# First expert of a retention and mixture-of-experts kernel: the order of its second half

## The chip, the cores and the metric

One core of a Trainium2 chip runs the whole program. The metric is the device time of one execution in microseconds (us). A core has TensorE (PE in the rows; PEld is its weight load), VectorE (DVE), ScalarE (ACT), GpSimd (POOL) and SyncE (SP). SP and POOL also issue the transfers here: SP the plain loads and the transpositions, POOL the indirect gathers and scatters.

## What is computed

```python
def _attn_ref(q, k, v):                    # B, H, S, D = 8, 8, 576, 64
    scores = np.matmul(q, k.transpose(0, 1, 3, 2)) / np.sqrt(D)
    gamma = 1.0 - 2.0 ** (-5.0 - np.arange(H))
    rel = pos[:, None] - pos[None, :]
    Dmat = np.where(rel >= 0, gamma[:, None, None] ** rel[None, :, :], 0.0)
    return np.matmul(scores * Dmat[None], v)

def _moe_ref(x, expert_emb, tau, w1, w2):  # N, D, E, F = 4608, 512, 8, 1024
    xn, en = rows of x and expert_emb divided by (norm + 1e-6)
    logits = xn @ en.T / tau
    expert_idx = argmax(logits, axis=1)
    probs = softmax(logits)
    for e in range(E):
        mask = expert_idx == e
        h = np.maximum(x[mask] @ w1[e], 0.0)
        out[mask] = probs[mask, e, None] * (h @ w2[e])
```

The result of the retention, with the heads side by side, is x. Each token goes to one expert, and its row is scaled by that expert's probability, the gate.

## The kernel before, in words

All is in one function, `retention_moe`. The retention runs first and writes x to a table in HBM (xd). Routing gives every expert five tiles of 128 slots (0 to 4). For an expert e the tokens' rows are gathered by an indirect transfer (`gather`, L379), turned by a DMA transposition on SP's queue (`turn`, L405) and put together from 16-bit halves on ScalarE (`join`, L416). The gates are gathered by five more indirect transfers, 128 numbers each (`gather_gates`, L392), from a table gd that `gates_out` (L254) writes through SP.

Numbers are 32 bits wide, and TensorE multiplies in a reduced form. So every operand is split into a high part (ScalarE copies and rounds it: `whi` L989 and `Split.hi` for weights, `xhi0` L429 and `xhi` L461 for x, `out0_hi` L997 for the middle layer) and a remainder (VectorE subtracts: `wlo` L992, `Split.lo`, `xlo0` L433, `xlo` L466, `out0_lo` L1001), and a product is three matmuls: high by high, high by low, low by high. `mm` (L127) issues all of them.

Expert 0 computes its first product directly: `mm1_in` (L471) makes one of eight groups of 128 columns of the middle layer, 12 matmuls, for tiles 0 to 2 first (q = 0) and then, once their x is there, for tiles 3 and 4 (q = 1, 256 columns). The second product, `mm2` (L1066), takes 24 matmuls of 512 columns a tile, called in pairs of groups; `evac` (L1081) scales the tile by its gates on ScalarE and `scatter` (L1087) writes it on POOL's queue. Experts 1 to 7 run in a loop (from L1296) and compute the first product by seven products of combined quarters (`products`, L1048). Their operands are sums of quarters of w1 (S1 to S4, `sumS1` and so on on VectorE, L977 to L987) and of x (`xsums`, L449), split like the rest. The quarter loads of w1 are `wload` (L963); `wn.load` brings w2, 512 KB a piece.

The order is written out by hand: inside `manual_schedule` every engine issues its instructions in the order of the program's text, and an instruction that waits holds everything behind it on its engine or queue. Lines on different engines don't order each other; only data and free buffers do. So the place of a line in the text counts only among the lines of the same engine. Buffers that matter here: `graw` has three (a turn of tiles 3 and 4 of expert 1 takes one as well), `wraw` has three for all weight loads, PSUM banks pa hold the groups of `mm1_in` in turn (four), and ys two.

The stretch that the change touches is L1133 to L1266: the end of expert 0's first part (L1133 to L1157), tiles 0 and 1 of its second product with the preparation of tiles 3 and 4 among them (L1160 to L1193), the second part of its first product (the loop at L1194), and tiles 2 to 4 of the second product (L1211 to L1266), beside which expert 1's x and weights are got ready. `sum_beyond` (L510) adds up, in 14 small instructions on VectorE, how many tiles the overflow code at the end has to treat; its result is read only by expert 7's turn of the loop (L1299) and behind it.

Of the kernel before, what the change touches and what calls it, by code (L numbers as in the profile page):

```python
# [97 lines left out]
def retention_moe(ctx: ExitStack, tc: tile.TileContext, qk, kv, embT, tau, w1, w2, cst, out):  # L98
# [155 lines left out]
    def gates_out():  # L254

        ps = psm.tile([P, 512], F32, name="m")
        tr(ps[:, :P], tok_all, ident)
        rows = my.tile([P, DM], F32, name="y")
        nc.vector.tensor_copy(rows[:NT, :P], ps[:NT, :P])
        nc.sync.dma_start(out=gd[:, :].rearrange("(t p) o -> t (p o)", p=P), in_=rows[:NT, :P])  # L260
# [115 lines left out]
    xg, gts = {}, {}  # L376
# [15 lines left out]
    def gather_gates(e, tiles=range(CT)):  # L392
        if e not in gts:
            gts[e] = mg.tile([P, CT], F32, name="gt")
        g = gts[e]
        for i in tiles:
            a = _slot(e, i)
            nc.gpsimd.indirect_dma_start(  # L398
                out=g[:, i : i + 1],
                out_offset=None,  # L400
                in_=gd[:, :],
                in_offset=bass.IndirectOffsetOnAxis(ap=gid[:, a : a + 1], axis=0),
            )

    def turn(e, i):  # L405

        if e and i > 2:
            t, u = gr.tile([P, RW], F32, name="graw"), (gx, xsf[:, 2 * NP * HW :])[i - 3]
            xg[e, i] = t
        else:  # L410
            t = u = xg[e, i]
        nc.sync.dma_start_transpose(
            out=t[:, XO : XO + DM].bitcast(U16).rearrange("p (c n) -> p c n", n=P), in_=u[:, :DM].bitcast(U16)
        )

    def join(e, i, copy=nc.scalar.copy):  # L416

        t = xg[e, i]
        copy(  # L419
            t[:, :DM].bitcast(U16).rearrange("p (n h) -> p h n", h=2),  # L420
            t[:, XO : XO + DM].bitcast(U16).rearrange("p (h n) -> p h n", h=2),
        )
# [6 lines left out]
    def xhi0(i):  # L429
        u, x = rows0(i)  # L430
        nc.scalar.copy(x[:, 0], u)  # L431
# [495 lines left out]
    with ExitStack() as moe:  # L927
# [35 lines left out]
        def wload(e, n):  # L963

            i, j = int(n[1]) - 1, int(n[2]) - 1
            t = raw[n] = wr.tile([P, RW], F32, name="wraw")[:, :1024].rearrange("p (d n) -> p d n", d=2)
            nc.sync.dma_start(
                out=t,
                in_=w1[e][j * 256 : (j + 1) * 256, i * 512 : (i + 1) * 512].rearrange("(d p) n -> p d n", p=P),
            )  # L970
# [18 lines left out]
        def whi(n):  # L989
            nc.scalar.copy(wop[n][:, 0], raw[n])  # L990

        def wlo(n):  # L992
            nc.vector.tensor_tensor(  # L993
                out=wop[n][:, 1], in0=raw[n], in1=wop[n][:, 0].bitcast(F32), op=ALU.subtract
            )

        def out0_hi(f, q, ps):  # L997
            o, n = ((0, C0), (C0, C1))[q]
            nc.scalar.activation(hs[:, 0, f, o : o + n], ps[:, :n], AF.Relu)
# [66 lines left out]
        def mm2(ps, i, fs, n=0, step=DM, begin=None, end=None):  # L1066

            for f in fs:
                for k, (a, c) in enumerate(((0, 0), (0, 1), (1, 0))):
                    mm(  # L1070
                        ps[:, :step],
                        hs[:, a, f, i * P : (i + 1) * P],
                        w2t[:, c, f, n : n + step],
                        start=(f == begin and k == 0),
                        stop=(f == end and k == 2),
                        skip_group_check=True,
                    )
# [55 lines left out]
        mm1_in(5, 0, q0[5])  # L1133
        out0_hi(4, 0, q0[4])
        out0_lo(4, 0, q0[4])
        wn.lo(1)
        turn(0, 3)
        wload(1, "A11")
        mm1_in(6, 0, q0[6])
        on(prow)  # L1140
        gates_out()
        gather_gates(0)
        turn(0, 4)
        out0_hi(5, 0, q0[5])
        wn.hi(2)
        out0_lo(5, 0, q0[5])
# [12 lines left out]
        on(prow)  # L1159
        mm2(b0[0], 0, (0, 1), begin=0)  # L1160
        count_beyond()
        whi("A11")
        mm2(b0[0], 0, (2, 3))
        wlo("A11")
        join(0, 3)
        mm2(b0[0], 0, (4, 5))
        xhi0(3)
        join(0, 4)
        xlo0(3)
        xg.pop((0, 3))  # L1170
        gather(1, 1)
        gather(1, 4)
        mm2(b0[1], 1, (0, 1), begin=0)
        xhi0(4)
        sumS3()
        mm2(b0[1], 1, (2, 3))
        xlo0(4)
        xg.pop((0, 4))
        sumS1()
        mm2(b0[0], 0, (6, 7), end=7)  # L1180
        evac(0, 0, b0[0])
        scatter(0, 0)
        whi("S3")
        gather(1, 2)
        turn(1, 1)
        mm2(b0[1], 1, (4, 5))
        wlo("S3")
        whi("A22")
        gather_gates(1)
        mm2(b0[1], 1, (6, 7), end=7)  # L1190
        evac(0, 1, b0[1])
        scatter(0, 1)
# [1 line left out]
        for f in range(NF):  # L1194
            ps = pa[f % 4]
            mm1_in(f, 1, ps)
            out0_hi(f, 1, ps)
            if f in (2, 4, 6):
                join(1, f // 2 - 1)
            if f in (3, 5, 7):  # L1200
                xsums(1, f // 2 - 1)
            out0_lo(f, 1, ps)
            if f in (3, 5, 7):
                xhi(1, f // 2 - 1, "a")
            if f in (4, 6):
                xlo(1, f // 2 - 2, "a")
            if f == 1:
                wlo("A22")
        sumS2("A22")
        wload(1, "A12")  # L1210
        mm2(b0[2], 2, (0, 1), begin=0)  # L1211
        xhi(1, 0, "bc")
        xlo(1, 2, "a")
        xlo(1, 0, "bc")
        xg.pop((1, 0))
        turn(1, 3)
        mm2(b0[2], 2, (2, 3))
        xhi(1, 1, "bc")
        xlo(1, 1, "bc")
        xg.pop((1, 1))  # L1220
        turn(1, 4)
        mm2(b0[2], 2, (4, 5))
        whi("S1")
        wlo("S1")
        wn = Split(1, 1, w2f)
        wn.load(0)
        mm2(b0[2], 2, (6, 7), end=7)
        evac(0, 2, b0[2])
        scatter(0, 2)
        xhi(1, 2, "bc")  # L1230
        mm2(b0[3], 3, (0, 1), begin=0)
        whi("A12")
        xlo(1, 2, "bc")
        xg.pop((1, 2))
        mm2(b0[3], 3, (2, 3))
        whi("S2")
        wlo("A12")
        sumS4()
        mm2(b0[3], 3, (4, 5))
        join(1, 3)  # L1240
        wlo("S2")
        wn.load(1)
        mm2(b0[3], 3, (6, 7), end=7)
        evac(0, 3, b0[3])
        scatter(0, 3)
        xhi(1, 3, "ab")
        xsums(1, 3)
        mm2(b0[4], 4, (0, 1), begin=0)
        xhi(1, 3, "c")
        join(1, 4)  # L1250
        xlo(1, 3, "abc")
        xg.pop((1, 3))
        mm2(b0[4], 4, (2, 3))
        xhi(1, 4, "ab")
        xsums(1, 4)
        sum_beyond()
        mm2(b0[4], 4, (4, 5))
        xhi(1, 4, "c")
        whi("S4")
        xlo(1, 4, "abc")  # L1260
        xg.pop((1, 4))
        mm2(b0[4], 4, (6, 7), end=7)
        evac(0, 4, b0[4])
        scatter(0, 4)
        wlo("S4")
        wn.load(2)  # L1266


        def outs_mid(fs, X, Y):
# [26 lines left out]
        for e in range(1, NE):  # L1296
# [151 lines left out]
            if more:  # L1448
                wlo("S4")
                wnext.load(2)  # L1450
            mm2(o[3], 3, (6, 7), end=7)
            evac(e, 3, o[3])
            scatter(e, 3)
# [7 lines left out]
            wn = wnext  # L1461
# [174 lines left out]
```

## Time and profile before

| | us |
|---|---|
| three runs | 580.13, 582.66, 584.71 |
| median | 582.66 |
| the profiled execution's own time | 582.66 |
| its span, first to last instruction | 580.8 |
| TensorE busy in it | 560.1 (96%) |
| VectorE, ScalarE, POOL busy | 402.2, 353.2, 207.4 |
| mean granted clock of TensorE | 0.991 |

Times inside the span are counted from its start. The first expert's stretch runs from about 154 to 223, each later expert takes some 50. In a timeline a row gives start, length, engine, line, operation, what it writes and reads, shapes and count, and in brackets how long the engine stood idle before it and what ended that. "issue" is a wait for nothing that the profile shows. [...] Ends of matmuls are modelled, their starts are recorded.

### The profile page before, as it was taken

What the parts mean: (1) busy time and instruction counts of PE and PEld (TensorE: products, weight loads), DVE (VectorE), ACT (ScalarE), POOL (GpSimd) and SP (SyncE); (2) the same over time, 40 slices, a digit from 0 to 9 for tenths busy, and PEclk for the clock granted to TensorE, in tenths of its full rate; (3) what the DMA queues carried; (4) which work ended last, traced back from release to release, by engine and by line L of the source; (5) the groups of instructions that cost most, each with busy time, mean ns of one, the idle gap of its engine ahead of it and who ended that gap; (6) DMA issues with size and microseconds to landing.
All of it is one profiled execution on the core that took longest, in us unless ns stands there. A gap on an engine that the chain in (4) does not pass through costs nothing.

```text
span 580.8 us, 13121 instructions
## 1 busy us (share of the span) xinstructions
PE 560.1 (96%) x5156; PEld 502.5 (87%) x5156; DVE 402.2 (69%) x880; ACT 353.2 (61%) x640; POOL 207.4 (36%) x188
## 2 busy tenths in 40 slices
PE   8999999998999898999999999999999999999995
PEld 7888888887897778988998998899799889889985
DVE  2776787877686486896698488669868848975400
ACT  2344355553665377676778578677877856776411
POOL 3763333217343715006504611640570362070021
PEclk9999999999999989999999999999999999999998
DMA  8999999999358545936744593584575459262011
GB/s 294 417 356 365 343 358 357 373 322 196 122 167 196 127 128 189 205 74 181 227 92 138 191 212 87 169 249 84 146 243 121 109 166 273 71 163 84 2 45 41
DMA packets 83067, 111.53 MB, mean 192 GB/s; under 512 B 48135, under 2 KB 48427, under 8 KB 82992
## 3 DMA queue, kind: packets, MB, share of 16 engines
q1 hardware_dynamic: 75312, 90.55, 52.7%
q0 software_dynamic: 7680, 19.95, 10.4%
q8 instruction: 51, 0.84, 0.6%
q14 instruction: 24, 0.20, 0.1%
HBM read 81.10 MB, written 19.94 MB: 174 GB/s over the span
## 4 chain that ended last, share of the span: by engine, by line
PE 71%; issue 11%; DVE 8%; ACT 5%; DMA 2%; POOL 2%; POOLq 0%; ACTq 0%; SPq 0%
PE pa L127 27%; PE po L127 21%; PE pst L127 14%; PE prow L127 7%; PE pa L131 2%; ACT graw L419 2%; PE prow L131 1%; DMA graw<-graw 1%; DVE graw L454 1%; POOL out L1089 1%; DVE w0f L993 1%; DMA graw<-xd,gid 1%; DVE pm L662 1%; DVE hs L1022 1%; ACT w0f L990 1%
## 5 line engine op out<-in xcount | busy, mean ns | idle before, releaser
L1089 POOL DMA_INDIRECT out<-y,sid x40 | 42.5, 1063 | 237.6 <-ACT y L1085 217.0
L127 PE MATMUL po<-w2f,hs 128*128 128x512 f32 x408 | 97.4, 397 | 3.2 <-issue 3.2
L127 PEld LDWEIGHTS po<-w2f,hs 128*128 128x128 f32 x408 | 78.2, 192 | 20.6 <-issue 4.3
L127 PE MATMUL pst<-w2f,hs 128*128 128x512 f32 (+1 forms) x336 | 78.4, 382 | 0.0
L193 DVE TENSOR_TENSOR w2f<-wraw,w2f 128x1024 fp32r<-128x1024 f32 x32 | 39.3, 1227 | 53.4 <-ACT w2f L189 45.2
L127 PEld LDWEIGHTS pst<-w2f,hs 128*128 128x128 f32 x336 | 61.0, 188 | 11.4
L645 POOL TENSOR_TENSOR kvt<-kvt,cs 128x512 f32<-128x512 f32 x35 | 38.7, 1111 | 57.6 <-DMA kvt<-kv 52.7
L398 POOL DMA_INDIRECT gt<-gd,gid x40 | 50.2, 1255 | 20.1 <-issue 11.9
L419 ACT COPY graw<-graw 128x1024 uint16<-128x1024 uint16 x37 | 50.3, 1360 | 2.7 <-DMA graw<-graw 1.9
L127 PE MATMUL pa<-xxf,w0f 128*128 128x296 f32 (+2 forms) x348 | 50.3, 296 | 1.2 <-ACT xxf L431 0.9
L127 PEld LDWEIGHTS pa<-xxf,w0f 128*128 128x128 f32 x348 | 47.6, 188 | 1.9 <-ACT xxf L431 1.3
L662 DVE TENSOR_TENSOR pm<-pa,tri 128x512 f32<-128x512 f32 x64 | 40.1, 682 | 9.4 <-PE pa L127 9.3
L127 PE MATMUL prow<-w2f,hs 128*128 128x512 f32 x192 | 46.0, 389 | 0.0
L127 PE MATMUL pa<-qkt 64*128 64x128 f32 x576 | 42.3, 281 | 1.4 <-DVE t L295 0.7
L127 PEld LDWEIGHTS prow<-w2f,hs 128*128 128x128 f32 x192 | 36.0, 188 | 7.5
L385 POOL DMA_INDIRECT graw<-xd,gid x26 | 32.6, 1254 | 24.4 <-DVE L_all L799 13.6
L127 PEld LDWEIGHTS pa<-qkt 64*128 64x128 f32 x576 | 37.4, 187 | 4.1 <-DVE t L295 1.1
L464 ACT CAST xxf<-graw 128x128 fp32r<-128x128 f32 x70 | 31.7, 459 | 14.3 <-DVE graw L454 12.6
L454 DVE TENSOR_TENSOR graw<-graw 128x128 f32<-128x128 f32 x140 | 34.4, 286 | 7.8 <-ACT graw L419 6.6
L127 PE MATMUL pa<-xsf,w0f 128*128 128x296 f32 (+2 forms) x240 | 39.5, 315 | 0.0
L127 PEld LDWEIGHTS pa<-xsf,w0f 128*128 128x128 f32 x240 | 36.6, 189 | 0.3 <-DVE xsf L435 0.2
L127 PE MATMUL po<-pm,kvt 128*64 128x128 f32 (+1 forms) x640 | 34.9, 263 | 0.0
(196 smaller groups left out, 1102.1 us busy)
## 6 DMA issues: line engine op xcount, KB each, us to landing
wraw<-w SPq DMA_DIRECT2D x64, 512.0 KB
qkt<-qk SPq DMA_DIRECT2D x36, 512.0 KB
kvt<-kv SPq DMA_DIRECT2D x32, 512.0 KB
xd<-xw SPq DMA_DIRECT2D x36, 256.0 KB
kvt<-kv SPq DMA_DIRECT2D x4, 256.0 KB
gt<-gd,gid POOLq DMA_INDIRECT x40
out<-y,sid POOLq DMA_INDIRECT x40
graw<-xd,gid POOLq DMA_INDIRECT x26
```

The costliest lines, as they stand in the source:

```text
L127: pe[:] = [nc.tensor.matmul(*args, **kw)]
L131: pe[:] = [nc.tensor.transpose(*args, **kw)]
L193: nc.vector.tensor_tensor(out=self.to[:, 1, c * 1024 : (c + 1) * 1024], in0=self.raws.pop(c), in1=hi.bitcast(F32), op=ALU.subtract,)
L385: return nc.gpsimd.indirect_dma_start(out=t[:, :DM].bitcast(U16), out_offset=None, in_=xd[:rows, :], in_offset=bass.IndirectOffsetOnAxis(a ...
L398: nc.gpsimd.indirect_dma_start(out=g[:, i : i + 1], out_offset=None, in_=gd[:, :], in_offset=bass.IndirectOffsetOnAxis(ap=gid[:, a : a + 1 ...
L419: copy(t[:, :DM].bitcast(U16).rearrange("p (n h) -> p h n", h=2), t[:, XO : XO + DM].bitcast(U16).rearrange("p (h n) -> p h n", h=2),)
L454: nc.vector.tensor_tensor(out=v[:, 2 * k : 2 * k + 2], in0=a, in1=b, op=ALU.subtract)
L464: nc.scalar.copy(x[:, 0], u)
L645: eng.tensor_tensor(out=v, in0=v, in1=gneg[:, t % KT].unsqueeze(2).broadcast_to([P, H, D]), op=ALU.mult)
L662: nc.vector.tensor_tensor(out=pm[:, h], in0=banks[h].rearrange("p (c n) -> p c n", c=NP), in1=m.unsqueeze(1).broadcast_to([P, NP, P]), op= ...
L990: nc.scalar.copy(wop[n][:, 0], raw[n])
L1089: sc = nc.gpsimd.indirect_dma_start(out=out[:, :], out_offset=bass.IndirectOffsetOnAxis(ap=sid[:, a : a + 1], axis=0), in_=ys[i], in_offse ...
```

## The change

Nothing that is computed changes; no instruction is added or left out. Lines move:

- In the first part `wn.lo(1)` goes behind `gates_out()`, and the load of A11 for expert 1 behind `turn(0, 4)`.
- Among tiles 0 and 1 of the second product the joins and splits of tiles 3 and 4 go ahead of the splits of A11, `gather(1, 2)` and `turn(1, 1)` ahead of the first scatter, and `gather_gates(1)` leaves.
- In the second part of the first product only tile 0 of expert 1 is joined and summed; `sumS2`, the load of A12 and tile 0's remainder come earlier.
- Among tiles 2 to 4 of the second product tiles 1 and 2 of expert 1 are joined, summed and split, then tiles 3 and 4 as later experts do it; S2's split comes earlier, `wn.load(0)` now ahead of `turn(1, 4)`.
- The gates of expert 1 are gathered behind the scatters of tiles 3 and 4, and `sum_beyond` runs in the loop at e = 1, behind `wlo("S4")`.

```diff
--- before.py
+++ after.py
@@ -1133,14 +1133,14 @@
         mm1_in(5, 0, q0[5])
         out0_hi(4, 0, q0[4])
         out0_lo(4, 0, q0[4])
-        wn.lo(1)
         turn(0, 3)
-        wload(1, "A11")
         mm1_in(6, 0, q0[6])
         on(prow)
         gates_out()
+        wn.lo(1)
         gather_gates(0)
         turn(0, 4)
+        wload(1, "A11")
         out0_hi(5, 0, q0[5])
         wn.hi(2)
         out0_lo(5, 0, q0[5])
@@ -1159,34 +1159,33 @@
         on(prow)
         mm2(b0[0], 0, (0, 1), begin=0)
         count_beyond()
-        whi("A11")
+        join(0, 3)
         mm2(b0[0], 0, (2, 3))
-        wlo("A11")
-        join(0, 3)
-        mm2(b0[0], 0, (4, 5))
         xhi0(3)
         join(0, 4)
         xlo0(3)
         xg.pop((0, 3))
         gather(1, 1)
         gather(1, 4)
+        mm2(b0[0], 0, (4, 5))
+        xhi0(4)
+        whi("A11")
+        xlo0(4)
+        xg.pop((0, 4))
+        gather(1, 2)
         mm2(b0[1], 1, (0, 1), begin=0)
-        xhi0(4)
+        wlo("A11")
         sumS3()
         mm2(b0[1], 1, (2, 3))
-        xlo0(4)
-        xg.pop((0, 4))
+        whi("S3")
+        turn(1, 1)
         sumS1()
         mm2(b0[0], 0, (6, 7), end=7)
         evac(0, 0, b0[0])
         scatter(0, 0)
-        whi("S3")
-        gather(1, 2)
-        turn(1, 1)
         mm2(b0[1], 1, (4, 5))
         wlo("S3")
         whi("A22")
-        gather_gates(1)
         mm2(b0[1], 1, (6, 7), end=7)
         evac(0, 1, b0[1])
         scatter(0, 1)
@@ -1195,75 +1194,80 @@
             ps = pa[f % 4]
             mm1_in(f, 1, ps)
             out0_hi(f, 1, ps)
-            if f in (2, 4, 6):
-                join(1, f // 2 - 1)
-            if f in (3, 5, 7):
-                xsums(1, f // 2 - 1)
+            if f == 2:
+                join(1, 0)
+            if f == 3:
+                xsums(1, 0)
             out0_lo(f, 1, ps)
-            if f in (3, 5, 7):
-                xhi(1, f // 2 - 1, "a")
-            if f in (4, 6):
-                xlo(1, f // 2 - 2, "a")
             if f == 1:
                 wlo("A22")
-        sumS2("A22")
-        wload(1, "A12")
+            if f == 4:
+                xhi(1, 0, "a")
+            if f == 5:
+                sumS2("A22")
+                wload(1, "A12")
+                xlo(1, 0, "a")
         mm2(b0[2], 2, (0, 1), begin=0)
         xhi(1, 0, "bc")
-        xlo(1, 2, "a")
         xlo(1, 0, "bc")
         xg.pop((1, 0))
         turn(1, 3)
+        join(1, 1)
         mm2(b0[2], 2, (2, 3))
-        xhi(1, 1, "bc")
-        xlo(1, 1, "bc")
-        xg.pop((1, 1))
-        turn(1, 4)
-        mm2(b0[2], 2, (4, 5))
+        xsums(1, 1)
         whi("S1")
+        xhi(1, 1, "abc")
         wlo("S1")
         wn = Split(1, 1, w2f)
         wn.load(0)
+        xlo(1, 1, "abc")
+        xg.pop((1, 1))
+        turn(1, 4)
+        join(1, 2)
+        mm2(b0[2], 2, (4, 5))
+        whi("S2")
+        xsums(1, 2)
+        xhi(1, 2, "abc")
+        wlo("S2")
+        xlo(1, 2, "abc")
+        xg.pop((1, 2))
         mm2(b0[2], 2, (6, 7), end=7)
         evac(0, 2, b0[2])
         scatter(0, 2)
-        xhi(1, 2, "bc")
         mm2(b0[3], 3, (0, 1), begin=0)
         whi("A12")
-        xlo(1, 2, "bc")
-        xg.pop((1, 2))
-        mm2(b0[3], 3, (2, 3))
-        whi("S2")
         wlo("A12")
         sumS4()
+        wn.load(1)
+        join(1, 3)
+        mm2(b0[3], 3, (2, 3))
+        xhi(1, 3, "ab")
+        xsums(1, 3)
         mm2(b0[3], 3, (4, 5))
-        join(1, 3)
-        wlo("S2")
-        wn.load(1)
+        join(1, 4)
+        xlo(1, 3, "ab")
+        xhi(1, 3, "c")
+        xhi(1, 4, "ab")
+        xsums(1, 4)
+        xlo(1, 3, "c")
+        xg.pop((1, 3))
         mm2(b0[3], 3, (6, 7), end=7)
         evac(0, 3, b0[3])
         scatter(0, 3)
-        xhi(1, 3, "ab")
-        xsums(1, 3)
-        mm2(b0[4], 4, (0, 1), begin=0)
-        xhi(1, 3, "c")
-        join(1, 4)
-        xlo(1, 3, "abc")
-        xg.pop((1, 3))
-        mm2(b0[4], 4, (2, 3))
-        xhi(1, 4, "ab")
-        xsums(1, 4)
-        sum_beyond()
-        mm2(b0[4], 4, (4, 5))
+        gather_gates(1, (0, 1, 2))
         xhi(1, 4, "c")
-        whi("S4")
         xlo(1, 4, "abc")
         xg.pop((1, 4))
+        mm2(b0[4], 4, (0, 1), begin=0)
+        mm2(b0[4], 4, (2, 3))
+        whi("S4")
+        wlo("S4")
+        wn.load(2)
+        mm2(b0[4], 4, (4, 5))
         mm2(b0[4], 4, (6, 7), end=7)
         evac(0, 4, b0[4])
         scatter(0, 4)
-        wlo("S4")
-        wn.load(2)
+        gather_gates(1, (3, 4))
 
 
         def outs_mid(fs, X, Y):
@@ -1448,6 +1452,8 @@
             if more:
                 wlo("S4")
                 wnext.load(2)
+            if e == 1:
+                sum_beyond()
             mm2(o[3], 3, (6, 7), end=7)
             evac(e, 3, o[3])
             scatter(e, 3)
```

## Rows read from the trace of the kernel before

**Rows 1.** Waits of TensorE over the span: in total, times, longest (us).
```profile
PE po L127 <- issue: 3.4, 6, 1.4
PE pa L127 <- DVE xsf L469: 1.9, 1, 1.9
```

**Rows 2.** Timeline of TensorE: start, length, engine, what [idle before].
```profile
143.39 1.10 PE L127 MATMUL po<-qkt,T 64*64 64x128 f32 x32
...
174.40 1.55 PE L127 MATMUL po<-w2f,hs 128*128 128x512 f32 x6
...
186.54 0.38 PE L127 MATMUL pa<-xxf,w0f 128*128 128x256 f32 x1 [0.90 <-ACT xxf L431]
187.26 11.42 PE L127 MATMUL pa<-xxf,w0f 128*128 128x256 f32 x95 [0.34 <-DVE xxf L435]
198.94 0.40 PE L127 MATMUL po<-w2f,hs 128*128 128x512 f32 x1 [0.26 <-issue]
...
203.86 6.89 PE L127 MATMUL po<-w2f,hs 128*128 128x512 f32 x19 [1.36 <-issue]
210.58 5.62 PE L127 MATMUL pst<-w2f,hs 128*128 128x512 f32 x24
...
221.48 0.31 PE L127 MATMUL pa<-xsf,wxf 128*128 128x320 f32 x1
223.69 1.88 PE L127 MATMUL pa<-xsf,wxf 128*128 128x320 f32 x11 [1.89 <-DVE xsf L469]
```

**Rows 3.** Busy time by stretch: length, engines, granted clock (PEclk), DMA share.
```profile
198.70:210.60 11.90, 8.75 (x25) 6.22 (x25) 6.65 (x19) 5.77 (x12) 2.75 (x3) 0.71 0.22 53
210.60:221.50 10.90, 10.90 (x50) 9.00 (x48) 9.29 (x21) 8.92 (x15) 2.13 (x2) 1.00 0.80 229
221.50:223.70 2.20, 0.31 (x3) 0.01 (x1) 1.89 (x12) 1.56 (x3) 0.36 (x1) 1.00 0.00 0
```

The engines stand in the order PE, PEld, DVE, ACT, POOL.

**Rows 4.** Timeline of ScalarE.
```profile
181.62 1.05 ACT L990 CAST wxf<-wraw 128x1024 fp32r<-128x1024 f32 x1 [6.09 <-DMA wraw<-w]
182.57 1.36 ACT L419 COPY graw<-graw 128x1024 uint16<-128x1024 uint16 x1
...
184.48 1.35 ACT L419 COPY graw<-graw 128x1024 uint16<-128x1024 uint16 x1
...
203.89 0.38 ACT L999 ACTIVATE hs<-pa 128x256 fp32r<-128x256 f32 x1 [4.53 <-remote]
```

**Rows 5.** Timeline of VectorE.
```profile
189.89 0.42 DVE L1003 SCALAR_TENSOR_TENSOR hs<-pa,hs 128x256 fp32r<-128x256 f32 x1 [0.41 <-ACT hs L999]
...
221.59 1.52 DVE L517 TENSOR_TENSOR ovs<-ovs,ovf 128x1 f32<-128x1 f32 x8
...
223.22 0.42 DVE L469 TENSOR_TENSOR xsf<-graw,xsf 128x256 fp32r<-128x256 f32 x1
...
277.99 1.23 DVE L193 TENSOR_TENSOR w2f<-wraw,w2f 128x1024 fp32r<-128x1024 f32 x1 [6.79 <-ACT w2f L189]
```

**Rows 6.** The chain that ended last, 170 to 230: start, length, what.
```profile
174.83 7.69 DMA graw<-graw
```

**Rows 7.** Timeline of POOL.
```profile
182.11 0.95 POOL L398 DMA_INDIRECT gt<-gd,gid  x1 [8.20 <-DMA gd<-y]
...
194.80 0.95 POOL L398 DMA_INDIRECT gt<-gd,gid  x1 [0.30 <-issue]
...
201.05 1.01 POOL L1089 DMA_INDIRECT out<-y,sid  x1 [0.30 <-issue]
...
224.80 1.65 POOL L385 DMA_INDIRECT graw<-xd,gid  x1 [0.30 <-DVE xxf L469]
```

**Rows 8.** Timeline of SP's queue.
```profile
236.78 6.12 SPq L412 DMA_TRANSPOSE graw<-graw  x3
```

**Rows 9.** Groups of VectorE, 186 to 224, by shape: count, busy us, mean ns.
```profile
L454 DVE TENSOR_TENSOR graw<-graw 128x128 f32<-128x128 f32 x20 | 5.0, 289 | 3.4 <-ACT graw L419 3.2
...
L993 DVE TENSOR_TENSOR w0f<-wraw,w0f 128x1024 fp32r<-128x1024 f32 x3 | 3.7, 1220 | 0.4 <-ACT w0f L990 0.4
```

## The prediction

> **What bounds the kernel now.** The waits of TensorE come first. The reader is to see how few there are: over the whole span the longest groups are 3.4 us that end with "issue" and 1.9 us behind VectorE's remainders of xsf [rows 1]. Both lie where the diff works, the first expert's second half. The second view is TensorE's timeline of that stretch [rows 2]. It begins at 174.40 with the second product (24 matmuls of 512 columns a tile, 48 for tiles 0 and 1). A tile in the clear takes from 210.58 to about 216.03, 5.45 us or 0.227 us a matmul, so tiles 0 and 1 are through at 174.40 + 48 x 0.227 = 185.3, with a matmul of count_beyond at about 185.5. The second part of the first product (96 matmuls) could start there. TensorE issues one at 186.54 and the other 95 from 187.26; at 11.2/95 = 0.1175 us each, 96 could end at 185.5 + 11.3 = 196.8 and end at 198.5: 1.7 us lost. Tile 2 should take 5.45 us and takes from 198.5 to 210.58, 12.1 us: 6.6 us lost, part because five matmuls (24 less 19) trickle out between 198.94 and 203.86, part because the 19 from 203.86 take 6.89 us, 0.36 us each. The products of expert 1 begin with one matmul at 221.48 and the other eleven at 223.69: 2.1 us. In all 10.4 us.
>
> [...] Fourth, ScalarE [rows 4] and VectorE [rows 5]. ScalarE stands in whi("A11") until 181.62, and only then, in its order, come the joins and splits of tiles 3 and 4, which the waiting product reads. Its evacuation of the sixth of the eight groups (203.89) has waited 4.53 us, though by TensorE's rows that group was issued by 187.26 + 71 x 0.1175 = 195.6. So TensorE is held from inside the 96 matmuls on, by something that no row names.
>
> **Part 1, joins of expert 0 before whi("A11"); wn.lo(1), A11's load and the gates.** Before, the chain stands 7.69 us behind tile 4's transposition [rows 6], whose data lies behind A11's load in SP's queue; A11's 512 KB land first (181.62) and the join starts after its split, at 182.57 [rows 4]. Afterwards the load is issued behind the transposition. From the start of tile 4's join (184.48) to the 95 matmuls (187.26) it takes 2.8 us. If the transposition lands no earlier than 182.5, and the join of tile 3 is done by then, the product can start at 185.3, before 185.5; with A11's data out of the way it lands earlier. So the 1.7 us go in either case. Bounds: 0 (the transposition late by as much) to 1.7; I take 1.7, the row being that of the chain itself. VectorE does the gates' copy before wn.lo(1) and so three evacuations some 0.6 us later (an estimate); the second product reads the last of them only with tile 0's last pair, at 174.4 + 30 x 0.227 = 181.2, some 4 us later: nothing, or 0.6 if that cover is gone. whi("A11") now waits for a load that is one transposition later (about 2 us, from 236.78 and 6.12 us for three [rows 8]), and whi("S3"), evac(0, 0), whi("A22") and the first relu stand behind it. That relu's remainder now starts at 189.89 [rows 5]; with four banks TensorE needs the first bank back at 185.5 + 4 x 1.41 = 191.1. Slack 0.8 us; cost 0, at worst 1.
>
> **Part 2, joins, sums and splits of expert 1.** Before, three joins lie inside the 96 matmuls; afterwards one. The splits go to tiles 2 to 4 of the second product. Between the end of the 96 and expert 1's products each engine has this to do: VectorE was busy 6.65 + 9.29 + 1.89 = 17.8 us from 198.70 to 223.70, of which the three last remainders (1.3), sumS2 (1.2) and sum_beyond (2.3) go elsewhere: 13.0. ScalarE was busy 5.77 + 8.92 + 1.56 = 16.3, less three relus (1.2) and whi("S4") (1.0), which the first product pair doesn't need: 14.1. TensorE has 3 x 5.45 = 16.4. From the release at 203.9 to 223.2 the two needed 19.3 us for about 16.6 busy, a share of 0.86; so 13.0 becomes 15.1 and 14.1 becomes 16.4: a tie with TensorE. As tile 4's join, sums, split and remainder alternate between the two engines, I take a wait of 1.0 us at expert 1's first product, between 0 and 4 (the boundary's 2.1 doubled). On SP, turn(1, 4) is now behind wn.load(0), 512 KB, which waits for wlo("S1"). It waits for tile 1's remainders: from 197 on a join of 1.36 us, four sums of 0.29, wlo("S1") of 1.22 [rows 9] and the remainders around them, so it is issued near 202.7 (an estimate); its join is wanted once ScalarE has done two joins and three splits more, near 208. Those 5 us hide it, if the transposition takes less.
>
> **Part 3, expert 1's gates behind the last scatters.** Before, five gathers of gates from 194.80 to 200.74, 1.25 us each, lie beside the 96 matmuls [rows 7]. Afterwards POOL has there only three gathers of x and two scatters; the fifth gather of x runs before the first scatter, and turn(1, 1) and turn(1, 2) follow it. The gates get 3 places behind scatter(0, 3) and 2 behind scatter(0, 4), so POOL's queue holds scatter(0, 4) and expert 2's five gathers by up to 5 x 1.25 = 6.3 us. Those gathers start at 224.80, 1.3 us after the products, and the transposition that reads the first starts only at 236.78 [rows 7, 8]. Some 10 us of cover: nothing, or what exceeds it.
>
> What the trickle is worth hangs on this part, and the trace before has no row for its cause. Bounds: 6.6 us (it goes) to 0 (it stays), and below 0 if it grows (rival 3). For its going: it occurs once, where gates, transpositions of x and the fast matmuls come together; it ends at 203.86, about 2 us after POOL's last instruction of that burst; the other gate gathers, from 182.11 on, lie beside the slow matmuls, and expert 1's gathers of x beside products without a trickle. In the new order POOL's burst is five instructions of 1.25 us beside the 96 matmuls instead of ten. I take 6.6.
>
> [...]
>
> **Part 4, sum_beyond a stage later.** Eight additions of 1.52 us from 221.59 on and six small ones, some 2.3 us in all, stood ahead of tile 4's remainder at 223.22, for which the products wait [rows 5]: 2.1 us go. Behind expert 1's wlo("S4") VectorE has 6.79 us idle up to 277.99; the 2.3 us fit. Cost 0, 2.3 if that cover were gone. What is late next is the wait of part 2.
>
> **Sum.** 1.7 + 6.6 + 2.1 - 1.0 = 9.4 us. The profiled execution took 582.66 us, span 580.8 and 1.9 around it, and is the median of the three runs shown. Everything behind expert 1's first product is TensorE back to back, so the gain is kept: 582.7 - 9.4 = 573.3 us.
>
> **Rivals.**
> 1. The trickle doesn't hang on the gates and stays; the change does not do what it might. If the sixth of the eight groups is again released about 1.7 us earlier than now, 202.2, the last remainders and sumS2 are done near 205, and 13.0 and 14.1 us at a share of 0.86 put the products at 220.3 instead of 223.6: 3.3 us, 579.4. For it: DMA is at 0.22, so no transfer stands in the way, and the transpositions still run beside the fast matmuls. Against: the list above.
> 2. The end of ScalarE's queue becomes the bound: turn(1, 4) behind wn.load(0) takes the 7.69 us of the chain's row instead of the 5 that are hidden, and wn.load(0) as much as 1.5 ahead of it. Its join stands ahead of tile 4's splits and evac(0, 3): 4.2 us more at the products, 577.5; with a stretch at the lower clock (19 x (0.36 - 0.23) = 2.6 us) 580.1.
> 3. Slower: the trickle grows. The transpositions come earlier and nearer together, and if the second product issues all of tile 2 in the way that five matmuls show now (4.92/5 = 0.98 us instead of 0.227), tile 2 takes 23.6 us instead of 12.1; less the 3.3 of rival 1 that is 8.2 us lost, 590.9. It decides from a trickle 3.3 us longer than now, some four or five matmuls more. For it: nothing names the cause. Against: fewer POOL instructions and a burst that ends earlier.
>
> **How the numbers follow.** The forecast has 0.55, rival 1 0.28, rival 2 0.10, rival 3 0.07. About 1% (5.8 us) is what a measurement of this kernel can tell from no change. The forecast is faster by more; of rival 1 some 0.06 (a trickle that shrinks); rivals 1 and 2 else lie within: faster 0.61, same 0.32, slower 0.07. The range begins with no wait at the boundary and 1.8 us for runs (the runs shown differ by about 2 us from their median): 570.5. It ends with rivals 1 and 2: 580.5.
>
> **What would show it.** Right: the 96 matmuls start by 185.7 in one piece; ScalarE's joins of tiles 3 and 4 stand before A11's split; tile 2 takes 5.5 us, with no clock under 1.00 up to expert 1; the products start between 213 and 215; sum_beyond fills idle time behind expert 1's wlo("S4"). Wrong: a trickle with "issue" beside the transpositions, a second stretch at 0.5, a product that waits over 3 us for xsf, or expert 2's joins waiting for late gathers.

## The result, and the profile after

The changed kernel takes 574.54 us (median of 4 runs, 573.13 to 576.07), the kernel before 582.34 us (4 runs, 580.13 to 584.71): ratio 0.9854, 95% interval 0.9815 to 0.9894, so 7.8 us faster. The forecast was 573.3 us. The sum was nearly right, in part by luck; the experiments show that its terms were not, since two of the obstacles stand side by side in time and can't be added.

The profiled execution took 576.07 us (span 574.3), the highest of its four. First TensorE's waits (total, times, longest, us), where [rows 1] stood:

```profile
PE pa L127 <- issue: 2.1, 4, 0.9
...
PE po L127 <- issue: 0.9, 3, 0.4
```

The wait for VectorE's xsf is gone, and that with "issue" at po is down from 3.4 to 0.9, none of it in this stretch. Of the 2.1 us at pa, 1.2 us (0.53 + 0.20 + 0.43) stand in the 96 matmuls of 256 columns; the fourth wait lies far ahead of them. TensorE's timeline, beside [rows 2]:

```profile
176.12 1.55 PE L127 MATMUL po<-w2f,hs 128*128 128x512 f32 x6
...
187.20 6.61 PE L127 MATMUL pa<-xxf,w0f 128*128 128x256 f32 x55
194.34 0.53 PE L127 MATMUL pa<-xxf,w0f 128*128 128x256 f32 x3 [0.53 <-issue]
195.07 0.28 PE L127 MATMUL pa<-xxf,w0f 128*128 128x256 f32 x1 [0.20 <-issue]
195.78 4.87 PE L127 MATMUL pa<-xxf,w0f 128*128 128x256 f32 x37 [0.43 <-issue]
200.49 5.61 PE L127 MATMUL po<-w2f,hs 128*128 128x512 f32 x24
205.93 5.60 PE L127 MATMUL pst<-w2f,hs 128*128 128x512 f32 x24
...
216.81 1.92 PE L127 MATMUL pa<-xsf,wxf 128*128 128x320 f32 x12
...
220.34 1.92 PE L127 MATMUL pa<-xsf,w0f 128*128 128x320 f32 x12
```

The second product starts 1.72 us later than before (176.12 against 174.40). Most of that arose in the retention, where this execution ran some microseconds at the lower clock; it isn't owed to the change: the start lies between 171.74 and 177.03 in the fourteen traces of this document. The busy time by stretch (length, busy time of PE, PEld, DVE, ACT, POOL, granted clock, DMA share, GB/s), of the kernel before and then of the changed one:

```profile
9.00:13.00 4.00, 3.83 (x77) 3.33 (x75) 1.29 (x2) 0.99 (x3) 3.88 (x6) 1.00 1.02 388
```

```profile
9.00:13.00 4.00, 4.00 (x44) 3.48 (x48) 1.01 (x2) 0.50 (x2) 3.44 (x5) 0.57 0.94 343
...
187.20:200.49 13.29, 12.14 (x98) 11.58 (x96) 8.70 (x15) 6.95 (x13) 5.47 (x6) 1.00 0.58 139
200.49:216.81 16.32, 16.32 (x74) 13.52 (x73) 15.43 (x39) 15.29 (x25) 2.78 (x3) 1.00 0.53 146
```

The change does not touch that stretch, so all that follows counts from the start of the second product, in three pieces: (a) to the first of the 96 matmuls of the first product's second part; (b) from there to the start of tile 3, which holds the 96 and tile 2; (c) from tile 3 to the third group of expert 1's products (220.34 above; 227.17 before). Undisturbed they take 11.08, 16.73 and 14.41 us, 42.2 in all (e5 below, which has no wait in them).

Before it was 12.14, 24.04 and 16.59 us; after it is 11.08, 18.73 and 14.41. The gain is 1.1 + 5.3 + 2.2 = 8.55 us. Behind the third group 353.6 us were left of the span before (580.8 less 227.17) and 354.0 now: nothing that was moved back costs more than 0.4 us there.

A trickle, matmuls that come singly or by twos and threes with waits for "issue" between them, is still there, but inside the 96 matmuls, shorter and without the low clock of [rows 3] (0.71 in that stretch of before, 0.50 from 203 to 208; here PEclk 1.00 in both stretches). From 200.49 TensorE is busy 16.32 of 16.32 us. ScalarE and VectorE work beside it (15.29 and 15.43): the tie that the prediction described, just won. ScalarE, beside [rows 4]:

```profile
180.84 1.35 ACT L419 COPY graw<-graw 128x1024 uint16<-128x1024 uint16 x1 [3.86 <-DMA graw<-graw]
...
184.66 1.04 ACT L990 CAST wxf<-wraw 128x1024 fp32r<-128x1024 f32 x1
...
195.87 0.39 ACT L999 ACTIVATE hs<-pa 128x256 fp32r<-128x256 f32 x1 [1.82 <-remote]
...
201.68 1.35 ACT L419 COPY graw<-graw 128x1024 uint16<-128x1024 uint16 x1
```

The joins of expert 0 come first and A11's split after them, and the join of expert 1's tile 1 (201.68) no longer waits for anything. VectorE has the sums of the overflow in expert 1, inside idle time, where [rows 5] had them at 221.59:

```profile
267.01 1.52 DVE L517 TENSOR_TENSOR ovs<-ovs,ovf 128x1 f32<-128x1 f32 x8
...
271.16 1.29 DVE L193 TENSOR_TENSOR w2f<-wraw,w2f 128x1024 fp32r<-128x1024 f32 x1 [2.44 <-ACT w2f L189]
```

### The profile page after: what moved, and what is told of

Same layout as the page of the kernel before. It is cut to its first block, busy times and chain, and to the rows that moved or that the text cites. A ratio compares the mean times of both kernels' runs of the same rounds, so it can differ in the third digit from the quotient of the medians.

```text
span 574.3 us, 13123 instructions
## 1 busy us (share of the span) xinstructions
PE 559.5 (97%) x5156; PEld 503.1 (88%) x5156; DVE 404.2 (70%) x880; ACT 352.1 (61%) x640; POOL 207.7 (36%) x188
## 4 chain that ended last, share of the span: by engine, by line
PE 75%; issue 11%; DVE 7%; ACT 3%; POOL 1%; DMA 1%; POOLq 0%; ACTq 0%; DVEq 0%; SPq 0%
PE pa L127 27%; PE po L127 22%; PE pst L127 15%; PE prow L127 8%; PE pa L131 2%; PE prow L131 1%; DMA graw<-graw 1%; DVE graw L454 1%; POOL out L1089 1%; ACT graw L419 1%; DVE w0f L993 1%; DVE pm L662 1%; DVE hs L1022 1%; DVE st L1035 1%; ACT w0f L990 1%
## 5 line engine op out<-in xcount | busy, mean ns | idle before, releaser
L127 PE MATMUL po<-w2f,hs 128*128 128x512 f32 x408 | 94.1, 389 | 0.0
L127 PEld LDWEIGHTS po<-w2f,hs 128*128 128x128 f32 x408 | 76.4, 188 | 15.7
L645 POOL TENSOR_TENSOR kvt<-kvt,cs 128x512 f32<-128x512 f32 x35 | 37.5, 1078 | 58.3 <-DMA kvt<-kv 49.5
```

The source lines that it names most:

```text
L127: pe[:] = [nc.tensor.matmul(*args, **kw)]
L645: eng.tensor_tensor(out=v, in0=v, in1=gneg[:, t % KT].unsqueeze(2).broadcast_to([P, H, D]), op=ALU.mult)
```

## The experiments

Twelve kernels ran in three groups, each group on one chip beside the kernel before. The table gives the pieces (a), (b), (c) of each profiled execution as defined above (us, each the difference of two starts in TensorE's timeline), and the median time against that of before in the same group. The kernel before was traced once, with the result and not in the groups, so its row of pieces is one execution's.

| kernel | (a) | (b) | (c) | sum | us | before | ratio, interval |
|---|---|---|---|---|---|---|---|
| undisturbed | 11.08 | 16.73 | 14.41 | 42.2 | | | |
| before | 12.14 | 24.04 | 16.59 | 52.8 | | | |
| changed | 11.08 | 18.73 | 14.41 | 44.2 | 574.54 | 582.34 | 0.9854 (0.9815-0.9894) |
| e1_gates_only | 11.09 | 16.73 | 24.64 | 52.5 | 582.78 | 583.36 | 0.9995 (0.9970-1.0021) |
| e2_gates_back | 11.08 | 24.69 | 14.41 | 50.2 | 581.60 | 583.36 | 0.9973 (0.9955-0.9990) |
| e3_turns_late | 11.08 | 18.18 | 17.37 | 46.6 | 578.09 | 583.36 | 0.9924 (0.9893-0.9955) |
| e4_scatters_late | 11.09 | 17.89 | 14.41 | 43.4 | 573.55 | 583.36 | 0.9833 (0.9800-0.9865) |
| e5_short_burst | 11.08 | 16.73 | 14.41 | 42.2 | 571.10 | 579.50 | 0.9848 (0.9783-0.9913) |
| e6_sum_back | 11.09 | 16.73 | 15.62 | 43.4 | 572.40 | 579.50 | 0.9878 (0.9812-0.9944) |
| e7_sum_only | 11.08 | 17.12 | 21.84 | 50.0 | 577.78 | 579.50 | 0.9967 (0.9932-1.0002) |
| e8_a11_first | 11.08 | 16.84 | 14.41 | 42.3 | 571.89 | 579.50 | 0.9856 (0.9791-0.9921) |
| e9_order_only | 11.09 | 27.13 | 15.62 | 53.8 | 582.92 | 584.02 | 0.9985 (0.9964-1.0005) |
| e10_after_again | 11.08 | 20.75 | 14.41 | 46.2 | 575.78 | 584.02 | 0.9848 (0.9807-0.9888) |
| e11_short_again | 11.08 | 16.74 | 14.40 | 42.2 | 572.50 | 584.02 | 0.9800 (0.9764-0.9836) |
| e12_turn_early | 11.40 | 25.39 | 18.92 | 55.7 | 583.83 | 584.02 | 0.9989 (0.9966-1.0012) |

**First group: is it the gates?** e1_gates_only is the kernel before with part 3 alone.

```diff
         whi("A22")
-        gather_gates(1)
...
         scatter(0, 3)
+        gather_gates(1, (0, 1, 2))
...
         scatter(0, 4)
+        gather_gates(1, (3, 4))
```

> The kernel before with one edit: expert 1's gates are gathered behind the scatters of tiles 3 and 4. Measure: from the first of the 95 fast matmuls to the end of tile 2, 23.3 us before, 18.7 us after, 16.7 in the clear. If the gates' gathers make the trickle: 17 to 19 us here, no second stretch at the lower clock, and 4 to 6 us off the time (577 to 578). If the transpositions or the gathers of x and the scatters make it: 21 us or more and a time within 2 us of before.

Measured: nothing gained. TensorE's timeline shows why:

```profile
186.52 11.43 PE L127 MATMUL pa<-xxf,w0f 128*128 128x256 f32 x96
...
218.41 0.64 PE L127 MATMUL pa<-xsf,wxf 128*128 128x320 f32 x1 [4.12 <-ACT xsf L464]
221.95 3.30 PE L127 MATMUL pa<-xsf,wxf 128*128 128x320 f32 x11 [2.90 <-DVE xsf L469]
225.05 3.00 PE L127 MATMUL pa<-xxf,w0f 128*128 128x320 f32 x12
```

The 96 matmuls run in one piece, as part 3 wanted. But the products of expert 1 now wait 4.12 and 2.90 us, and then run at the lower clock (11 in 3.30 us instead of 12 in 1.92). The granted clock by stretch:

```profile
216.00:228.00 12.00, 6.68 (x25) 6.34 (x26) 7.94 (x26) 6.81 (x11) 8.27 (x8) 0.57 0.43 124
```

All that (b) gained, (c) lost, a part of it as the lower clock behind the waits. What is late is on ScalarE, which stands in the join of tile 1 behind the fifth relu, with the last three relus and the rest of its work for expert 1 in its queue:

```profile
193.86 0.38 ACT L999 ACTIVATE hs<-pa 128x256 fp32r<-128x256 f32 x1 [0.74 <-PE pa L127]
199.26 1.36 ACT L419 COPY graw<-graw 128x1024 uint16<-128x1024 uint16 x1 [5.02 <-DMA graw<-graw]
```

In the kernel before the same join hardly waited, and what followed was the sixth relu's wait of [rows 4], for TensorE:

```profile
198.01 1.35 ACT L419 COPY graw<-graw 128x1024 uint16<-128x1024 uint16 x1 [0.82 <-issue]
```

Counted from the start of the second product the join comes at the same time in both, after 23.6 us before and 23.8 here. So the join comes no later with the trickle than without it; without it TensorE is early, and the join and what stands behind it are not.

e2_gates_back is the mirror of it: the changed kernel with the gates in their old place.

```diff
         whi("A22")
+        gather_gates(1)
...
-        gather_gates(1, (0, 1, 2))
...
-        gather_gates(1, (3, 4))
```

> The changed kernel with one edit: expert 1's gates gathered where they were, ahead of the scatter of tile 1. If the gates make the trickle: the same measure grows from 18.7 to 22 us or more, a stretch at the lower clock comes back, and the time goes to 578 or above. If not: 18 to 20 us and a time within 2 us of the changed kernel's 574.5.

The trickle is back, and no wait at the products:

```profile
188.11 6.40 PE L127 MATMUL pa<-xxf,w0f 128*128 128x256 f32 x51
...
200.64 6.88 PE L127 MATMUL pa<-xxf,w0f 128*128 128x256 f32 x35 [1.04 <-issue]
...
223.68 1.92 PE L127 MATMUL pa<-xsf,wxf 128*128 128x320 f32 x12
```

The same move of the gates is worth nothing in the old order (582.78 against 583.36) and 8.05 us in the new one (581.60 less 573.55, which e4 took).

e3_turns_late asks whether the transpositions beside the 96 matmuls make what is left of the trickle: those of tiles 1 and 2 go behind the load of A12.

```diff
-        turn(1, 1)
...
-        turn(1, 2)
...
             if f == 4:
                 xhi(1, 0, "a")
+            if f == 7:
+                turn(1, 1)
+                turn(1, 2)
```

> The changed kernel with one edit: the transpositions of tiles 1 and 2 of expert 1 are issued behind the load of A12, so when the 96 matmuls are nearly through. If the transpositions make what is left of the trickle: the measure falls from 18.7 to 17 us. If POOL's gathers and scatters do: it stays within 1 us of 18.7. The joins of tiles 1 and 2 come later in either case and may cost 1 to 3 us at expert 1's first product.

They don't: (b) is 18.18, and 17.89 in the repeat of the changed kernel on this chip (e4). But (c) lost 3 us, with 1.34 and 1.10 us of waits at the products; so the new order needs the early transpositions.

e4_scatters_late wrote the two scatters behind the loop and left the evacuations where they were.

```diff
-        scatter(0, 0)
...
-        scatter(0, 1)
...
+        scatter(0, 0)
+        scatter(0, 1)
         mm2(b0[2], 2, (0, 1), begin=0)
```

> The changed kernel with one edit: the scatters of tiles 0 and 1 are issued behind the whole first product, when the 96 matmuls are nearly through. If POOL's instructions hold TensorE as long as they last: the trickle ends some 2.5 us earlier and the measure falls from 18.7 to 17 or 17.5 us. If the gathers of x or the transpositions alone do: it stays near 18.7. Nothing waits for the scatters, so no other cost: 572 to 575 us.

POOL has nothing between them and that place and waits only for the evacuations; it issued them at 189.79 and 191.12, in the old time. The experiment says nothing of scatters, and stands as a repeat of the changed kernel (573.55 us).

**Second group, another chip: the parts one by one.** e5_short_burst moves the evacuations of tiles 0 and 1 as well, so that POOL has only three gathers of x beside most of the 96 matmuls.

```diff
-        evac(0, 0, b0[0])
-        scatter(0, 0)
...
-        evac(0, 1, b0[1])
-        scatter(0, 1)
...
                 xlo(1, 0, "a")
+                evac(0, 0, b0[0])
+                scatter(0, 0)
+        evac(0, 1, b0[1])
+        scatter(0, 1)
         mm2(b0[2], 2, (0, 1), begin=0)
```

> The changed kernel with one edit: tile 0 is evacuated and scattered at the sixth group of the 96 matmuls and tile 1 behind the loop, so POOL's unbroken burst ends with its fifth gather of x, some 2.5 us earlier. If POOL's back-to-back indirect transfers of any kind hold TensorE until about 1.5 us behind the last of them: the 96 matmuls come out in one piece (11.4 us instead of 13.3) and the time falls by 1 to 2 us, to 572.5 to 573.5. If only the gates' transfers do: no trickle should be left in the changed kernel either, which has one, so this theory expects nothing from the edit: 13.3 us again.

There is no trickle, but on this chip no kernel showed one (e6 and e8 have the burst of the changed kernel, e7 that of before), so this run alone proves nothing.

e6_sum_back puts the sums of the overflow back (part 4 undone), e7_sum_only does part 4 alone, and e8_a11_first puts the load and the split of A11 back ahead of the joins of expert 0 (part 1 undone).

```diff
         xsums(1, 4)
+        sum_beyond()
         xlo(1, 3, "c")
...
-            if e == 1:
-                sum_beyond()
```

> The changed kernel with one edit: sum_beyond again ahead of tile 4's last remainders in expert 0. The products start without a wait in the changed kernel, tile 4's first remainder is through 1.3 us ahead of them, so 2.3 us of sums should make them wait 0.5 to 1.5 us, and the time grow by as much (575 to 576). If the move is worth its full 2.1 us: 576.5 or more.

(c) grows by 1.2 us, a wait of the products:

```profile
211.70 1.88 PE L127 MATMUL pa<-xsf,wxf 128*128 128x320 f32 x11 [0.95 <-DVE xsf L469]
```

```diff
-        sum_beyond()
         mm2(b0[4], 4, (4, 5))
...
                 wnext.load(2)
+            if e == 1:
+                sum_beyond()
```

> The kernel before with one edit: sum_beyond in the loop at e = 1. If the 2.1 us at the boundary are its own: the products' wait falls from 1.9 to under 0.3 us and the time by 1.5 to 2.5 us against before (581). If ScalarE or another remainder is right behind it: less than 1 us.

The medians differ by 1.7 us, an interval that touches no change. The trace says more: the gates are in their old place and still (b) is 17.12. And, as in e1, the loss sits at the products, behind the join of tile 1 (TensorE, then ScalarE):

```profile
217.65 0.63 PE L127 MATMUL pa<-xsf,wxf 128*128 128x320 f32 x1 [4.03 <-ACT xsf L464]
```

```profile
198.38 1.35 ACT L419 COPY graw<-graw 128x1024 uint16<-128x1024 uint16 x1 [4.94 <-DMA graw<-graw]
```

So on this chip the old order loses 7.4 us in (c), with hardly any trickle to hide it.

```diff
+        wn.lo(1)
         turn(0, 3)
+        wload(1, "A11")
...
-        wn.lo(1)
         gather_gates(0)
         turn(0, 4)
-        wload(1, "A11")
...
         count_beyond()
+        whi("A11")
+        mm2(b0[0], 0, (2, 3))
+        wlo("A11")
         join(0, 3)
-        mm2(b0[0], 0, (2, 3))
...
-        whi("A11")
...
-        wlo("A11")
```

> The changed kernel with the order of before for A11: its load ahead of the gates and of turn(0, 4), its split ahead of the joins of tiles 3 and 4. If that order is what the 96 matmuls waited for: they start 1 to 2 us behind the second product again, POOL's burst begins later and reaches further into them, and the time grows by 1.5 to 4 us (576 to 578.5). If the start was late for another reason: within 1 us of 574.5.

(a) is 11.08, as with the change. So are e1, e7 and e9, which all have the old order of A11; only the profiled execution of before (12.14) and e12 (11.40) lost anything there. The trace also shows what the new order does for ScalarE. Its join of tile 1, which no longer waits, is

```profile
197.66 1.36 ACT L419 COPY graw<-graw 128x1024 uint16<-128x1024 uint16 x1
```

That is 23.6 us behind the start of the second product, against 24.0 in e7 on the same chip. The join is hardly earlier. But ScalarE has done all eight relus by then, against five in e7, and tile 3's join comes 5.6 us earlier (205.56 against 211.56, counted in the same way).

**Third group, a chip with the trickle: the order, and the burst.** e9_order_only is part 2 alone: the changed kernel with the edits of e2, e6 and e8 together.

> Part 2 alone: expert 1's gates, A11's order and sum_beyond stand as before; joins, sums, splits and gather(1, 2) as in the changed kernel. Theory now: this order carries the gain, since ScalarE no longer stands for some 5 us in tile 1's join with the sixth to eighth relu behind it. Then this kernel is 4 to 7 us faster than before, with the products of expert 1 waiting under 2 us, where the 96 matmuls run in one piece; with a trickle (gates in their old place) only 0 to 2 us faster, with tile 2 starting after 204. The prediction's theory: this part costs about 1.0 us by itself, so this kernel is 0 to 2 us slower than before.

1.1 us in the medians, with an interval that reaches past no change. TensorE, and POOL in the same stretch:

```profile
184.66 7.78 PE L127 MATMUL pa<-xxf,w0f 128*128 128x256 f32 x59
192.65 0.28 PE L127 MATMUL pa<-xxf,w0f 128*128 128x256 f32 x1 [0.22 <-issue]
193.37 0.63 PE L127 MATMUL pa<-xxf,w0f 128*128 128x256 f32 x3 [0.44 <-issue]
194.80 1.08 PE L127 MATMUL pa<-xxf,w0f 128*128 128x256 f32 x4 [0.80 <-issue]
196.94 0.77 PE L127 MATMUL pa<-xxf,w0f 128*128 128x256 f32 x2 [1.06 <-issue]
199.05 0.37 PE L127 MATMUL pa<-xxf,w0f 128*128 128x256 f32 x1 [1.34 <-issue]
...
201.87 4.63 PE L127 MATMUL pa<-xxf,w0f 128*128 128x256 f32 x24 [0.33 <-issue]
206.34 5.61 PE L127 MATMUL po<-w2f,hs 128*128 128x512 f32 x24
...
223.93 1.88 PE L127 MATMUL pa<-xsf,wxf 128*128 128x320 f32 x11 [0.95 <-DVE xsf L469]
```

```profile
190.99 1.02 POOL L1089 DMA_INDIRECT out<-y,sid  x1 [0.30 <-ACT hs L999]
192.31 1.02 POOL L398 DMA_INDIRECT gt<-gd,gid  x1 [0.30 <-DMA xsf<-xd,gid]
...
198.63 1.11 POOL L1089 DMA_INDIRECT out<-y,sid  x1 [0.30 <-issue]
```

The 96 matmuls take 21.7 us instead of 11.3; the trickle lasts while POOL sends gates and scatters and ends 2.1 us after the last of them (198.63 + 1.11 = 199.74). The waits at the products are down to 0.95 us, but the trickle has taken what that would give.

e10_after_again is the changed kernel once more, for a trace on this chip. Against it e9 differs in the gates, and also in the order of A11 and the place of the sums.

> The changed kernel without an edit, for a trace beside the others of this call. All theories: 0.981 to 0.989 of the kernel before. Open: whether the 96 matmuls run in one piece (tile 2 some 11.5 us behind their start) or with a trickle (12.4 to 13.3 us).

```profile
186.20 4.15 PE L127 MATMUL pa<-xxf,w0f 128*128 128x256 f32 x34
190.68 0.52 PE L127 MATMUL pa<-xxf,w0f 128*128 128x256 f32 x3 [0.32 <-issue]
...
193.73 7.91 PE L127 MATMUL pa<-xxf,w0f 128*128 128x256 f32 x56 [0.33 <-issue]
```

A trickle from some 190.4 to 193.7, and then a stretch at the lower clock (56 matmuls in 7.91 us, where 6.6 would do; the granted clock is 0.86 from 186 to 198, 1.00 after): 4.0 us lost in (b).

e11_short_again has the edit of e5, here.

> The changed kernel with the two evacuations and scatters of tiles 0 and 1 behind the 96 matmuls' fifth group and their end, so that POOL issues nothing but three gathers beside them. If POOL's indirect transfers make the trickle: where the unchanged copy in this call shows one, this kernel shows none and is 1 to 2 us faster; where the copy shows none, both take the same within 1 us. If something else makes it: a trickle here as well, and the same time.

```profile
185.98 11.43 PE L127 MATMUL pa<-xxf,w0f 128*128 128x256 f32 x96
197.25 5.63 PE L127 MATMUL po<-w2f,hs 128*128 128x512 f32 x24
```

```profile
188.67 0.94 POOL L385 DMA_INDIRECT graw<-xd,gid  x1 [0.30 <-issue]
195.87 1.63 POOL L1089 DMA_INDIRECT out<-y,sid  x1 [6.26 <-ACT y L1085]
```

No trickle, all three pieces undisturbed, and 3.3 us less than the unchanged copy beside it (575.78 less 572.50), about what (b) lost there. This version beats both kernels: 0.980 of before.

e12_turn_early leaves the joins in the 96 matmuls and has tile 2's gather ahead of the first scatter.

```diff
         gather(1, 4)
+        gather(1, 2)
...
+        turn(1, 1)
         sumS1()
...
-        gather(1, 2)
-        turn(1, 1)
```

> The kernel before with nothing but gather(1, 2) ahead of the first scatter and the transposition of tile 1 (turn(1, 1)) up to its new place; joins stay inside the 96 matmuls. If tile 1's join is late because its data is late, and that alone: 3 to 5 us faster than before, with ScalarE waiting under 2 us at that join. If it is the place of the joins in ScalarE's queue that counts: under 1 us, with the wait of 4 to 5 us at that join still there.

583.83 us, no gain; (c) is still 4.5 us too long with (b) 8.7 too long as well. ScalarE's waits here are those of relus, which read what TensorE writes, and not of the join for the transposition:

```profile
199.74 0.38 ACT L999 ACTIVATE hs<-pa 128x256 fp32r<-128x256 f32 x1 [5.50 <-remote]
...
203.63 1.35 ACT L419 COPY graw<-graw 128x1024 uint16<-128x1024 uint16 x1
```

So it can't say whether the earlier data alone would do without a trickle, the less as its edit left tile 1's transposition where it was in SP's queue: between the two places of turn(1, 1) stands nothing that SP issues. What the traces do say is that tile 1's join need not be earlier (e8 against e7) and must not be later: in e3 it comes at 203.40, 29.2 us behind that start, and (c) loses 3.0 us.

## Why the prediction was right, and where its sum was not

**The two obstacles stand side by side, and the sum added them.** In the old order either the trickle is there, and (b) loses 7.3 us and (c) 2.2 (before); or it isn't, and then tile 1's join, with relus behind it on ScalarE, makes (c) lose 7.4 us (e7) or 10.2 (e1). In both of these the matmuls behind the waits are a part of the loss: 11 take 3.30 us instead of 1.88, in e1 in a stretch with the granted clock at 0.57 (216 to 228). Tile 1's join comes 23.6 to 24.0 us behind the second product's start in before, e1 and e7; its work is done beside the trickle when there is one; take the trickle away and it stands on the path. One trace of the old order had both: e12, with a trickle that came earlier, lost 8.7 and 4.5. In the new order with its early transpositions (c) loses at most 1.2 us, and the trickle, if there is one, counts in full: 8.0 us (e2), 10.4 (e9). So part 3 alone gave 0.9995, part 2 alone 0.9985, and the whole 0.9854 and, again, 0.9848. The step that failed is "Part 3 ... I take 6.6" as a term that could be added by itself, and beside it "I take a wait of 1.0 us" for part 2. How much hangs on that shows where there is hardly a trickle: on the second group's chip the old order loses 0.4 us in (b) and 7.4 in (c) (e7), the new one 0.1 in all (e8). The gain there is the one that the prediction priced with 2.1 - 1.0 us, and the 6.6 are not there to be had.

**Its own signs.** The 96 matmuls started in time (187.20 less the 1.72 is 185.48), ScalarE's joins stood ahead of A11's split, tile 2 took 5.44 us, the clock stayed at 1.00 (it had been 0.50 from 203 to 208 before), and the products started at 215.1 by the same count (213 to 215 was forecast). But the 96 did not run in one piece, and a sign that it had listed under "wrong", a trickle with "issue" beside the transpositions, stood in the changed kernel's trace.

**Part 3.** For the new order on a chip with the trickle the size was right: with the gates back (b) is 24.69 instead of 17.89 us on the same chip, 6.8, about the upper bound. In the old order (b) fell too, to 16.73 (e1), but (c) took it back, and the lower bound (0) is what was measured. What is left of the trickle, 2.0 us in the changed kernel's trace, was not forecast.

**Part 2** was priced as a cost of 1.0 us. There is no wait: 12 matmuls at 216.81 in one piece. The tie of 16.4 us of TensorE with the two other engines was the right picture, but not by its numbers. The prediction counted 13.0 us of work for VectorE and 14.1 for ScalarE, and they did 15.43 and 15.29. The count was taken from 198.70 on, and tile 1's join, which moved in, began at 198.01 before. And its busy share of 0.86 was exceeded (15.43 of 16.32 is 0.95). What was overlooked is what the old order would have cost once the trickle had gone. No row of before says it: the wait of 4.53 us in [rows 4] is the sixth relu's, for TensorE, and tile 1's join waited 0.82.

**Part 1.** Predicted 1.7 us, and found between the two traces: 1.1 in (a), and 0.6 in (b), where the second of the 96 came 0.72 us behind the first (186.54 and 187.26 in [rows 2]) instead of 0.12. But it is not owed to the order of A11: e8 has the old order and loses nothing. The wait in [rows 2] was that of one execution. A late matmul in a single trace is no term of a sum until the next one shows it.

**Part 4.** Predicted 2.1 us against the wait before; between the two traces (c) gained 2.2. In the new order the sums by themselves are worth 1.2 us (e6, and e9 on another chip); the rest of their 2.3 us has cover there.

**Rivals.** The trickle that stays came in part true: 1.2 to 4.0 us lost in (b) in the changed kernel and its copies (e4, e10), not 6.6, and hardly any on the second group's chip (e6, e8). The one at the end of ScalarE's queue didn't come: tile 4's join waits for nothing. The longer trickle came only with the gates in place: 8.0 us in e2, 10.4 in e9, 8.7 in e12, against 7.3 before. The slower kernel that it would make did not follow even there: (a) and (c) gave back most of it, and e9's ratio is 0.9985.

**The 96 matmuls alone.** By themselves they make no trickle: four traces (e1, e5, e6, e11) have the same 96 in 11.43 us without a gap. What differs between e10 and e11 is when two evacuations and scatters come.

**Total.** Forecast a gain of 9.4 us; measured 8.55 in the stretch and 7.8 in the medians. That the two are so near is in part luck. The rest of the trickle took 1.9 of the 6.6 (5.3 in (b), less the 0.6 of part 1, is 4.7), the wait that didn't come gave 1.1 in (c), and 1.7 were the chance of one execution of before. With the rest of the trickle gone the time falls further, by 3.3 us from e10 to e11.

## What to carry to other kernels

Before a wait is priced, ask what runs beside it: work that is late by as much can stand in its place (from before to e1 (b) fell by 7.3 us and (c) grew by 8.05). Test such a change whole and in parts, as two edits that measure 0.9995 and 0.9985 alone gave 0.9854 here. And in an engine's queue, which here runs in program order, an instruction that waits for a transfer should not stand ahead of work that could be done meanwhile: in e7 ScalarE stood 4.94 us before tile 1's join, with three relus behind it. Where a trace shows a trickle beside a burst of indirect transfers, move a part of the burst and look again: on one of the chips here that was worth 3.3 us.

## What was not expected of the hardware

TensorE is held, in waits of up to 1.4 us with nothing but "issue" named, while POOL sends bursts of indirect transfers beside 256-column matmuls (in the kernel before it reaches into those of 512 columns). The last wait that TensorE's timeline shows in the hold ended behind POOL's last instruction of the burst in every trace that has a hold, by 0.3 us (e2, 200.64 less 200.34) to 2.1 us (e9); in the changed kernel it was 1.6 (195.78 less 194.19). And the hold grew with the burst: none with three gathers of x (e11), 4.0 us lost in (b) with two scatters more (e10), 10.4 with five gathers of gates as well (e9), all on one chip. A part of these losses is the lower clock behind the hold (0.86 from 186 to 198 in e10; 0.88 there and 0.70 from 198 to 210 in e9). That it depends on the burst and what came with it (the evacuations in e11; the order of A11 and the sums in e9) is shown on that chip; no run moves the scatters alone, and how they would hold TensorE is not shown. The burst isn't sufficient: e1 had the three gathers and two scatters and no hold, and e7 on another chip had everything and lost 0.4 us. Transfers of instructions are next to absent there: from 185 to 207, around e9's trickle, the DMA view has 2875 packets, 2874 of them in the two queues of the program's own transfers and one in a queue of the kind "instruction".

The starts that stand in e9's trickle come in steps: 192.65, 193.37, 194.80, 196.94, 199.05 are 0.72, 1.43, 2.14 and 2.11 us apart, all close to multiples of 0.71. Six of these matmuls take as much undisturbed (6 x 0.1175), but the step is not theirs, as the kernel before has it between matmuls of 512 columns (198.94 in [rows 2], then 0.71 us apart):

```profile
199.65 0.49 PE L127 MATMUL po<-w2f,hs 128*128 128x512 f32 x1 [0.32 <-issue]
200.36 0.40 PE L127 MATMUL po<-w2f,hs 128*128 128x512 f32 x1 [0.22 <-issue]
```

No run here says what sets that step.
